# Decode attention with a gated MLP on one core: the output summed transposed, wo on 32 partitions, and the last V in 64-row pieces

## The chip, the core and the metric

The kernel runs on one NeuronCore of a Trainium2 chip. The metric is the device time of one execution in microseconds (us). A core has a matrix engine (PE, whose weight loads the profile lists as PEld), a vector engine (DVE), a scalar engine (ACT), a general engine (POOL) and a queue engine (SP) that here issues transfers only. Sixteen DMA engines move data between HBM and the on-chip memory of 128 partitions; each engine works through its own packets in order.

## What is computed

The input is one token for each of two batches. A branch "a" is attention over a cache of 16,384 keys and values for 32 heads of 128 elements; a branch "b" is a mixer and an MLP; a gate mixes the two. With S = 1 the mixer's shifted groups are all zero, which the kernel uses (`shT` is zero).

```python
x = A_x                                            # 2 x 1 x 1024
g = sigmoid((x * gate_w).sum(-1, keepdims=True))
q = (x @ wq) by heads                              # 2 x 32 x 1 x 128
p = softmax(q k^T * 128**-0.5)                     # k_cache: 2 x 32 x 16384 x 128
a = (p @ v_cache) by heads @ wo                    # wo: 4096 x 1024
x1 = Bx + shifted(gelu(layernorm(Bx) @ w1)) @ w2
b = x1 + gelu(layernorm(x1) @ w3) @ w4             # w3: 1024 x 3584
out = g * a + (1 - g) * b                          # bf16
```

(The branch "b" is given x as its input.) K and V are 537 MB of the 573 MB that are read.

## The kernel before

**Units.** The work is cut into 32 units: 16 pairs of heads (`HP`) times two batches (`s`). A unit reads 8 MB of K and 8 MB of V, each in one transfer of 128 partitions with 65,536 B in each (`unit_rows`). The buffer `mem` has five cells of 32 KB a partition: K of batch 0 lies in cells 0 and 1, K of batch 1 in cells 1 and 2, V in cells 3 and 4. K of the next unit may be loaded when the half of K that shares its cell has been transposed (`tr3`), V when the product with the V before it is done (`pvd`).

**One unit.** DVE transposes K in eight chunks into two buffers `kt` (L631); PE multiplies each chunk with the stationary query in 8 matmuls (L654). DVE transposes the scores (L638) and takes the maximum (L640); ACT spreads it into a diagonal `Dm` (L668), PE sums that to all partitions (`R`, L666), DVE takes the bias `nb` (L689), ACT the exponent (L674), PE the sum (L692), DVE its reciprocal (L694). The product with V of the unit before (`pe_pv`, L699: 64 matmuls of 512 moving columns) stands between L666 and L692 on PE. `dve_rows` (L747, L753) folds its four blocks into `red`, two matmuls (L717) turn `red` into a column form `ot`, and DVE copies it to `OT` (L782).

**The projection.** After the unit of batch 1, `pe_project` (L732) multiplies with the 256 rows of wo that belong to the pair of heads. wo lies as `wo_t`, 128 partitions by 2 rows of 1,024; `OT` is stationary (2 columns), wo is moving, and the output accumulates in `arow` as four groups of two rows with 256 columns, over all 16 pairs. `wod` marks it done, and SP waits for that before it loads the next wo (L874).

**The order on the queues.** SP issues all large transfers, in program order, each behind its wait: in the loop (L858 and on, 15 passes) K of batch 0, V of batch 0, wo, K of batch 1, V of batch 1. V and wo belong to the pass before. Each engine runs its instructions in the order written, with waits on counting semaphores; no planner reorders them.

**Before the loop** the branch "b" is computed, its parts set between the first two units: wq, w1, w2, K, w3, K, w4 are loaded in this order; the GELU after w3 (`gelu_T`, L468 to L496) follows unit 0's softmax and sum; the product with w4 (L510) stands before the last chunk of unit 1's scores; then the first `pvd` and `wod` are given by PE (L839, L840) behind unit 1's sum, and four row adds (L845) make `brow`.

**After the loop** the last V of batch 1 comes in nine pieces (L898): seven of 32 rows of V in each partition and two of 16. The first three pieces go through the form with V moving (24 matmuls L699), the other 160 rows through a form with V stationary and two moving columns (L952). The last 256 rows of wo come as `wo_l` in two transfers (L905). Then follow `OTl` (L958), 8 projection matmuls (L963), the add of `brow` (L970) and two stores of 4 rows, one on SP and one on ACT (L973).

## Time and profile before

| what | value |
|---|---|
| runs | 1334.83, 1335.35, 1336.12 us; median 1335.35 |
| profiled execution | 1336.33 us, its span 1334.6 us |
| read from HBM | 572.53 MB, 429 GB/s over the span |
| busy | PE 748.9 us (56%), PEld 302.2 (23%), DVE 710.5 (53%), ACT 104.6 (8%), POOL 12.4 (1%) |
| K transposes, L631 | 256 of 2,283 ns |
| score matmuls, L654 | 2048 of 418 ns |
| PV matmuls, L699 | 2008 of 384 ns |
| projection matmuls, L732 | 120 of 314 ns |
| wo transfers | 15 of 512 KB, 28.5 us from issue to landing (median) |
| K and V transfers of 8 MB | 28.3 and 30.9 us from issue to landing (median) |

Busy times are added over instructions; PE's and PEld's overlap. The time from issue to landing holds the wait behind earlier transfers in the queue. The span is from the first to the last instruction of the profile.

### The profile page before, as it was taken

How to read it: one execution, taken by the hardware profiler on the slowest of the kernel's cores; microseconds unless marked ns; L12 is line 12 of the kernel's file. 1: busy time of each engine (PE TensorE's matmuls, PEld its weight loads, DVE VectorE, ACT ScalarE, POOL GpSimd, SP SyncE). 2: the span in 40 equal slices, each digit the busy share in tenths (PEclk: the TensorE clock that was granted, in tenths of full speed). 3: DMA queues.
4: the chain of work that ended last, by engine and by line, in shares of the span. 5: the costliest groups of instructions: out<-in, count | busy, mean ns of one | idle time of the engine just before them, and what ended most of it. 6: DMA issues, size and time to landing. Idle time of an engine off the chain costs nothing.

```text
span 1334.6 us, 11800 instructions
## 1 busy us (share of the span) xinstructions
PE 748.9 (56%) x4920; PEld 302.2 (23%) x4920; DVE 710.5 (53%) x712; ACT 104.6 (8%) x164; POOL 12.4 (1%) x44
## 2 busy tenths in 40 slices
PE   0655666554566555466654546655455665555664
PEld 0222222222222222222222212222222222222222
DVE  1465565654556654456565445655444656545561
ACT  0010000000000000000000000000000000000000
POOL 0000000000000000000000000000000000000000
PEclk9778887777888777788777788877778877777886
DMA  9999999999999999999999999999999999999997
GB/s 409 437 419 425 431 433 432 430 438 430 434 432 434 432 432 438 426 438 430 434 432 434 436 428 438 428 436 431 434 438 428 436 428 438 424 441 436 430 436 317
DMA packets 13993, 572.68 MB, mean 429 GB/s; under 512 B 1936, under 2 KB 1952, under 8 KB 4384
## 3 DMA queue, kind: packets, MB, share of 16 engines
q1 hardware_dynamic: 13544, 572.53, 99.5%
q8 instruction: 8, 0.13, 0.0%
q10 hardware_dynamic: 440, 0.01, 0.0%
q14 instruction: 1, 0.01, 0.0%
HBM read 572.53 MB, written 0.00 MB: 429 GB/s over the span
## 4 chain that ended last, share of the span: by engine, by line
DMA 65%; DVE 16%; PE 12%; issue 5%; SPq 1%; POOL 0%; ACT 0%; POOLq 0%; ACTq 0%
DMA mem<-in_A_k_cache_dram 64%; DVE kt L631 15%; PE S L654 11%; DMA wo_last<-in_A_wo_dram 2%; SPq L898 1%; PE oacc L699 0%; PE oacc L510 0%; ACT pt L674 0%; SPq L905 0%; SPq L869 0%; DVE x1row L809 0%; DVE st L638 0%; POOL ln_rstd L450 0%; POOL qw L265 0%; DVE tsc L823 0%
## 5 line engine op out<-in xcount | busy, mean ns | idle before, releaser
L654 PE MATMUL S<-kt,qw 128*128 128x512 bf16 x2048 | 548.9, 418 | 306.8 <-DVE kt L631 306.7
L631 DVE STREAM_TRANSPOSE kt<-mem 128x2048 f32<-128x2048 f32 x256 | 570.7, 2283 | 208.0 <-DMA mem<-in_A_k_cache_dram 154.6
L654 PEld LDWEIGHTS S<-kt,qw 128*128 128x128 bf16 x2048 | 196.3, 104 | 645.7 <-issue 338.9
L699 PE MATMUL oacc<-mem,pt 128*8 128x512 bf16 x2008 | 115.9, 384 | 4.0 <-DMA mem<-in_A_v_cache_dram 4.0
L674 ACT ACTIVATE pt<-st,nb 64x256 bf16<-64x256 f32 x64 | 89.7, 1401 | 226.0 <-DVE nb L689 225.5
L747 DVE TENSOR_SCALAR part<-oacc,maskr 128x128 f32<-128x128 f32 x31 | 10.9, 351 | 143.0 <-PE oacc L699 143.0
L668 ACT ACTIVATE Dm<-ident_s,m 128x128 f32<-128x128 f32 x32 | 12.8, 401 | 921.2 <-DVE m L640 921.2
L692 PE MATMUL tot<-rs,lmat 128*128 128x1 f32 x64 | 18.7, 362 | 105.3 <-ACT pt L674 105.3
L694 DVE RECIPROCAL rinv<-tot 128x1 f32<-128x1 f32 x32 | 5.4, 168 | 113.1 <-PE tot L692 113.1
L699 PEld LDWEIGHTS oacc<-mem,pt 128*8 128x8 bf16 x2008 | 46.2, 87 | 61.3 <-DMA mem<-in_A_v_cache_dram 4.1
L638 DVE STREAM_TRANSPOSE st<-S 128x512 f32<-128x512 f32 x32 | 22.9, 717 | 69.8 <-PE S L654 69.8
L717 PE MATMUL ot<-hsel,red 128*128 128x2 f32 x120 | 19.0, 263 | 54.7 <-DVE red L753 54.7
L666 PE MATMUL R<-Dm,ones_f 128*128 128x128 f32 x64 | 15.6, 326 | 54.4 <-ACT Dm L668 54.4
L692 PEld LDWEIGHTS tot<-rs,lmat 128*128 128x128 f32 x64 | 16.0, 311 | 112.3 <-ACT pt L674 112.3
L717 PEld LDWEIGHTS ot<-hsel,red 128*128 128x128 f32 x120 | 16.4, 196 | 69.8 <-DVE red L753 69.8
L674 ACT ACTIVATION_READ_ACCUMULATOR pt<-st,nb 64x1 f32 x64 | 30.6, 478 | 0.0
L666 PEld LDWEIGHTS R<-Dm,ones_f 128*128 128x128 f32 x64 | 9.5, 188 | 70.2 <-ACT Dm L668 70.2
L753 DVE SCALAR_TENSOR_TENSOR part<-oacc,maskr,part 128x128 f32<-128x128 f32 x62 | 21.7, 351 | 2.2
L782 DVE CAST OT<-ot 64x2 bf16<-64x2 f32 x60 | 9.6, 160 | 22.2 <-PE ot L717 21.8
L344 PE MATMUL tot<-zp,ones_f 128*128 128x2 f32 x2 | 0.6, 364 | 33.7 <-DVE zp L366 33.7
L615 POOL TENSOR_TENSOR qw<-qd,mask 128x16 bf16<-128x16 f32 (+1 forms) x32 | 8.4, 263 | 1138.6 <-PE S L654 1138.6
L689 DVE TENSOR_REDUCE nb<-R 64x1 f32<-64x64 f32 x64 | 14.2, 222 | 3.4 <-PE R L666 2.1
(104 smaller groups left out, 116.0 us busy)
## 6 DMA issues: line engine op xcount, KB each, us to landing
mem<-in_B_w_dram SPq DMA_DIRECT2D x2, 7168.0 KB, 27.6
wo<-in_A_wo_dram SPq DMA_DIRECT2D x15, 512.0 KB, 28.5
mem<-in_A_v_cache_dram SPq DMA_DIRECT2D x7, 1024.0 KB, 18.4
mem<-in_B_w_dram SPq DMA_DIRECT2D x2, 2048.0 KB, 29.3
mem<-in_A_v_cache_dram SPq DMA_DIRECT2D x2, 512.0 KB, 27.7
mem<-in_A_k_cache_dram SPq DMA_DIRECT2D x32, 28.3
wo_last<-in_A_wo_dram SPq DMA_DIRECT2D x2, 256.0 KB, 21.6
mem<-in_A_v_cache_dram SPq DMA_DIRECT2D x31, 30.9
```

The costliest lines, as they stand in the source:

```text
L631: DVE.transpose(out=kt[n % 2][:], in_=k_view(s)[:, c * CT : (c + 1) * CT, :].rearrange("p j d -> p (j d)").bitcast(FP32),).then_inc(S(f"tr ...
L638: DVE.transpose(out=st[:].rearrange("p j r -> p (j r)"), in_=sps[s][:]).then_inc(S("stT"), 1)
L654: ins = PE.matmul(sps[s][:].rearrange("p (j k) -> p j k", k=QP), lhsT=qw[s][:, v, NG - 1 - m : NG - 1 - m + P], rhs=ktb[:, half * GT : (ha ...
L666: PE.matmul(R_ps[:, 0:P], lhsT=ones_f[:], rhs=Dm[:], start=True, stop=True).then_inc(S("rr"), 1)
L668: ACT.activation(out=Dm[:], in_=ident_s[:], func=ACTF.Copy, scale=m_t[:, 0:1]).then_inc(S("dm"), 1)
L674: ins = ACT.activation(out=pts[s][rows, :, e, :].rearrange("p (m a) k -> p a k m", a=GT // 4), in_=st[rows, :, 0:NG].rearrange("p (a k) m ...
L689: ins = DVE.tensor_reduce(out=nb_t[rows], in_=R_ps[rows, rows], axis=AX.X, op=ALU.min)
L692: PE.matmul(tot_ps[:, 0:1], lhsT=lmat[:], rhs=rs_t[:], start=True, stop=True).then_inc(S("tt"), 1)
L699: ins = PE.matmul(oacc[s][QP * q : QP * q + 8, :], lhsT=pts[s][:, g].rearrange("p h k -> p (h k)"), rhs=V[:, 4 * g : 4 * g + 4, :].rearran ...
L717: ins = PE.matmul(ot_ps[:, 2 * r : 2 * r + 2], lhsT=red[:].rearrange("p e d -> p (e d)")[:, r : 2 * Dh : 2], rhs=hsel[:], start=True, stop ...
L753: ins = DVE.scalar_tensor_tensor(out=red[:] if twice else part[:], in0=in0.unsqueeze(1).to_broadcast([P, 2, Dh]) if twice else in0, scalar ...
L898: SP.dma_start(out=region(V_CELL, NJ * Dh)[:, at * Dh : (at + size) * Dh], in_=unit_rows(v_rows, HP - 1, 1)[:, at * Dh : (at + size) * Dh] ...
```

## The change

- wo lies on 32 partitions with 8 rows of 1,024 each (`WP` = 32, `WR` = 8), still 512 KB a transfer. The temporary `tsc` now shares its memory.
- The projection has wo stationary (every eighth column, 32 x 128) and `OT` moving (two columns): 64 matmuls for 8. `OT` is made by 8 matmuls instead of 2 and by two dependent DVE steps with a selector `esel`. The output accumulates transposed, 128 partitions by 8 by 2.
- `brow` is built in the same layout from `x1T`; xrow with its two loads, the row adds and some memsets go. One store on ACT writes the output, in pieces of 16 B.
- The last V comes in pieces of 64, 64, 64, 32, 16, 16 rows; the first three (192 rows) go through the moving form. `wo_l` lies in cell 2 and waits for the last transposes.
- `softmax` and `total` are split in five steps. In the loop their order on each engine stays; before the loop GELU comes ahead of unit 0's exponent, unit 0's sum stands amid unit 1's scores, `pvd` is given right behind the w4 product, and `wod` by DVE's step that makes `brow`.

```diff
-    wo_t = sb([P, 2, D], BF16, "wo")
-    wo_l = sb([P, 2, D], BF16, "wo_last")
+    wo_t = sb([P, WR, D], BF16, "wo")
+    wo_v = wo_t[0:WP].rearrange("p r (n c) -> p r c n", c=KC)
-    tsc = sb([P, HQ * Dh], FP32, "tsc")
+    tsc = wo_t[:, 0:2, :].rearrange("p r n -> p (r n)").bitcast(FP32)
...
-    wo_rows = A_wo.rearrange("(g p r) n -> g (p r n)", p=P, r=2)
+    wo_rows = A_wo.rearrange("(g p r) n -> g (p r n)", p=WP, r=WR)
...
         def pe_pv(u):
...
-            for r in range(2):
+            for r in range(WR):
                 ins = PE.matmul(
-                    ot_ps[:, 2 * r : 2 * r + 2],
-                    lhsT=red[:].rearrange("p e d -> p (e d)")[:, r : 2 * Dh : 2],
+                    ot_ps[0:WP, 2 * r : 2 * r + 2],
+                    lhsT=red[:].rearrange("p e d -> p (e d)")[:, r : 2 * Dh : WR],
...
         def pe_project(u):
...
-            for r in range(2):
-                for k in range(Q4):
+            for r in range(WR):
+                for c in range(KC):
                     ins = PE.matmul(
-                        arow[k],
-                        lhsT=OT[:, r, :],
-                        rhs=wo_t[:, r, k * NQ : (k + 1) * NQ],
+                        arow[:, c, :],
+                        lhsT=wo_v[:, r, c, :],
+                        rhs=OT[:, r, :],
...
         def dve_pv_end(u):
...
+            DVE.tensor_scalar(
+                out=oa[:], in0=ot[:, 0, :], scalar1=esel[:, 0:1], scalar2=None, op0=ALU.mult
+            ).then_inc(S("oad"), 1)
+            wait(DVE, "oad", u.after(-1))
             wait(DVE, "wod", u.i)
-            for e in range(2):
...
+            DVE.scalar_tensor_tensor(
+                out=OT[:, :, s], in0=ot[:, 1, :], scalar=esel[:, 1:2], in1=oa[:], op0=ALU.mult, op1=ALU.add
+            ).then_inc(S("OTd"), 1)
...
-        softmax(u0)
-        total(u0)
+        spread_max(u0)
...
         gelu_T(columns(FC), h2T[:], FC, "g2", "h2T")
+        bias(u0)
+        exponent(u0)
         pool_unit(u1)
-        dve_scores(u1)
-        pe_scores(u1, 0, NCK - 1)
+        dve_scores(u1, 0, NCK // 2)
+        pe_scores(u1, 0, NCK // 2 - 1)
+        total(u0)
+        invert(u0)
+        dve_scores(u1, NCK // 2)
+        pe_scores(u1, NCK // 2 - 1, NCK - 1)
         linear(h2T, w4_v, FC, D, "h2T", "c3", [ot_ps[:]], ["ot"])
-        pe_scores(u1, NCK - 1)
-        softmax(u1)
-        total(u1)
         ln.wait("PE", [ln.writer["ot"]])
         PE.sem_inc(S("pvd"), 1)
-        PE.sem_inc(S("wod"), 1)
+        pe_scores(u1, NCK - 1)
+        spread_max(u1)
+        bias(u1)
+        exponent(u1)
...
-                    SP.dma_start(out=wo_t[:].rearrange("p r n -> p (r n)"), in_=wo_source(i - 1)).then_inc(S("wol"), 16)
+                    SP.dma_start(out=wo_t[0:WP].rearrange("p r n -> p (r n)"), in_=wo_source(i - 1)).then_inc(S("wol"), 16)
...
-        PIECES = [32] * 7 + [16] * 2
+        PIECES = [64, 64, 64, 32, 16, 16]
...
+        wo_l = region(2, 2 * D).rearrange("p (e n) -> p e n", e=2)
+        wo_c = wo_l.rearrange("p e (n c) -> p e c n", c=KC)
+        wait(SP, f"tr{NCK - 1}", 2 * HP)
...
-            for k in range(Q4):
+            for c in range(KC):
                 ins = PE.matmul(
-                    arow[k], lhsT=OTl[:, e, :], rhs=wo_l[:, e, k * NQ : (k + 1) * NQ],
+                    arow[:, c, :], lhsT=wo_c[:, e, c, :], rhs=OTl[:, e, :],
...
-        for b, queue in ((0, SP), (1, ACT)):
...
+        ACT.dma_start(out=out.rearrange("b s (p c) -> p (b s) c", c=KC), in_=out_T[:]).then_inc(S("st"), 16)
```

More of the change, by code (lines that the diff above doesn't have):

```diff
@@ L127 @@
     HQ = H // Q4
+    WR = 8
+    WP = 2 * Dh // WR
     assert NCK == 8 and NG <= QP and FC * QP == FQ and KC * QP == NQ
@@ L144 @@
     kt = [sb([P, CT * Dh // 2], FP32, f"kt{k}") for k in range(2)]
-    wo_t = sb([P, 2, D], BF16, "wo")
-    wo_l = sb([P, 2, D], BF16, "wo_last")
+    wo_t = sb([P, WR, D], BF16, "wo")
+    wo_v = wo_t[0:WP].rearrange("p r (n c) -> p r c n", c=KC)
     st = sb([P, GT, QP], FP32, "st")
     Dm = sb([P, P], FP32, "Dm")
-    tsc = sb([P, HQ * Dh], FP32, "tsc")
+    tsc = wo_t[:, 0:2, :].rearrange("p r n -> p (r n)").bitcast(FP32)
     xin = sb([P, B, KC], BF16, "xin")
-    xrow = sb([P, NQ], BF16, "xrow")
     gwT = sb([P, KC], BF16, "gwT")
@@ L175 @@
     h2T = sb([P, FC, B], BF16, "h2T")
-    x1row = sb([P, NQ], FP32, "x1row")
-    brow = sb([P, NQ], FP32, "brow")
+    brow = sb([P, KC, B], FP32, "brow")
     g_rep = sb([P, B], FP32, "g_rep")
-    omgrow = sb([P, 1], FP32, "omgrow")
+    omg = sb([P, B], FP32, "omg")
+    esel = sb([WP, 2], FP32, "esel")
     m_t = sb([P, 1], FP32, "m")
@@ L188 @@
     red = sb([P, 2, Dh], FP32, "red")
-    OT = sb([P, 2, B], BF16, "OT")
+    oa = sb([WP, WR], FP32, "oa")
+    OT = sb([WP, WR, B], BF16, "OT")
     OTl = sb([P, 2, B], BF16, "OT_last")
-    out_row = sb([P, NQ], BF16, "out_row")
+    out_T = sb([P, B, KC], BF16, "out_T")
     sps = [psum.tile([P, GT * QP], FP32, name=f"S{k}") for k in range(2)]
@@ L195 @@
     oacc = [oacc2[:, k, :] for k in range(2)]
-    arow_t = psum.tile([P, NQ], FP32, name="arow")
-    arow = [arow_t[QP * k : QP * k + B, :] for k in range(Q4)]
+    arow = psum.tile([P, KC, B], FP32, name="arow")
     R_ps = psum.tile([P, 2 * P], FP32, name="R")
@@ L220, in wo_source @@
         flat = wo_rows[hp : hp + 1, :] if isinstance(hp, int) else wo_rows[bass.ds(hp, 1), :]
-        return flat.rearrange("o (p x) -> (o p) x", p=P)
+        return flat.rearrange("o (p x) -> (o p) x", p=WP)
     ln = Line(nc, S)
@@ L248 @@
         ln.dma("ACT", gwT[:], gate_w.rearrange("(p r) -> p r", p=P), "l_gw", writes=["gwT"])
-        for b in range(B):
-            ln.dma(
-                "ACT", xrow[b : b + QP * (Q4 - 1) + 1 : QP, :],
-                A_x[b, 0].rearrange("(k n) -> k n", k=Q4), f"l_xr{b}", writes=[f"xrow{b}"],
-            )
         ln.op("POOL", lambda: POOL.memset(ident_f[:], 0.0), writes=["ident"])
@@ L273 @@
         ln.op("DVE", lambda: DVE.memset(ot_ps[:], 0.0), writes=["ot"])
-        ln.op("DVE", lambda: DVE.memset(arow_t[:], 0.0), writes=["arow"])
         ln.op("DVE", lambda: DVE.memset(shT[:], 0.0), writes=["shT"])
-        ln.op("DVE", lambda: DVE.memset(brow[:], 0.0), writes=["brow"])
         ln.op("DVE", lambda: DVE.memset(hm2[:], 0.0), writes=["hm2"])
@@ L330 @@
         )
+        ln.op(
+            "DVE",
+            lambda: DVE.tensor_reduce(
+                out=esel[:], in_=ident_f[0:WP, 0:WP].rearrange("p (h k) -> p h k", h=2), axis=AX.X, op=ALU.add
+            ),
+            reads=["ident"], writes=["esel"],
+        )
         def many(count, make, reads, writes):
@@ L356, in compute_gate @@
             th = sb([P, B], FP32, "th")
-            om = sb([P, B], FP32, "om")
             ln.op(
@@ L383, in compute_gate @@
                 lambda: DVE.tensor_scalar(
-                    out=om[:], in0=g_rep[:], scalar1=-1.0, scalar2=1.0, op0=ALU.mult, op1=ALU.add
+                    out=omg[:], in0=g_rep[:], scalar1=-1.0, scalar2=1.0, op0=ALU.mult, op1=ALU.add
                 ),
-                reads=["g_rep"], writes=["om"],
-            )
-            ln.op(
-                "DVE",
-                lambda: DVE.tensor_tensor(out=om[:], in0=om[:], in1=rep1[:, 0:B], op=ALU.mult),
-                reads=["om", "rep1"], writes=["om"],
-            )
-            ln.op(
-                "DVE", lambda: DVE.tensor_reduce(out=omgrow[:], in_=om[:], axis=AX.X, op=ALU.add),
-                reads=["om"], writes=["omgrow"],
+                reads=["g_rep"], writes=["omg"],
             )
@@ L573 @@
         many(
-            Q4,
-            lambda g: PE.matmul(
-                arow[g],
-                lhsT=shT[:, 0, :],
-                rhs=rep4[:].rearrange("p g m -> p (g m)")[:, 0:NQ],
+            1,
+            lambda n: PE.matmul(
+                arow[:].rearrange("p c b -> p (c b)"),
+                lhsT=rep4[:, 0, :],
+                rhs=shT[:].rearrange("p c b -> p (c b)"),
                 start=True,
@@ L661, in pe_scores, with spread_max, exponent @@
                 ins.then_inc(S(f"sc{n}"), 1)
-        def softmax(u):
-            s = u.s
+        def spread_max(u):
+            wait(ACT, "mx", u.after(1))
+            ACT.activation(out=Dm[:], in_=ident_s[:], func=ACTF.Copy, scale=m_t[:, 0:1]).then_inc(S("dm"), 1)
             wait(PE, "dm", u.after(1))
             PE.matmul(R_ps[:, 0:P], lhsT=ones_f[:], rhs=Dm[:], start=True, stop=True).then_inc(S("rr"), 1)
-            wait(ACT, "mx", u.after(1))
-            ACT.activation(out=Dm[:], in_=ident_s[:], func=ACTF.Copy, scale=m_t[:, 0:1]).then_inc(S("dm"), 1)
+        def exponent(u):
+            s = u.s
             wait(ACT, "nbd", u.after(1))
@@ L682, in softmax, with bias @@
             ins.then_inc(S("ex"), 1)
-        def total(u):
-            s = u.s
+        def bias(u):
             wait(DVE, "rr", u.after(1))
@@ L690, in total, with invert @@
             ins.then_inc(S("nbd"), 1)
+        def total(u):
             wait(PE, "ex", u.after(1))
             PE.matmul(tot_ps[:, 0:1], lhsT=lmat[:], rhs=rs_t[:], start=True, stop=True).then_inc(S("tt"), 1)
+        def invert(u):
             wait(DVE, "tt", u.after(1))
-            DVE.reciprocal(out=rinv[s][:], in_=tot_ps[:, 0:1]).then_inc(S("rcp"), 1)
+            DVE.reciprocal(out=rinv[u.s][:], in_=tot_ps[:, 0:1]).then_inc(S("rcp"), 1)
         def pv_moving(V, s, g0, g1, ng):
@@ L778, in dve_pv_end @@
             wait(DVE, "otd", u.after(-1))
-            wait(DVE, "wod", u.i)
-            for e in range(2):
-                rows = slice(e * HALF, (e + 1) * HALF)
-                ins = DVE.tensor_copy(
-                    out=OT[rows, :, s],
-                    in_=ot_ps[rows, 0:4].rearrange("p (r e) -> p e r", e=2)[:, e],
-                )
-            ins.then_inc(S("OTd"), 1)
+            ot = ot_ps[0:WP, 0 : 2 * WR].rearrange("p (r e) -> p e r", e=2)
+            DVE.tensor_scalar(
+                out=oa[:], in0=ot[:, 0, :], scalar1=esel[:, 0:1], scalar2=None, op0=ALU.mult
+            ).then_inc(S("oad"), 1)
+            wait(DVE, "oad", u.after(-1))
+            wait(DVE, "wod", u.i)
+            DVE.scalar_tensor_tensor(
+                out=OT[:, :, s], in0=ot[:, 1, :], scalar=esel[:, 1:2], in1=oa[:], op0=ALU.mult, op1=ALU.add
+            ).then_inc(S("OTd"), 1)
         w3_v = region(3, KC * F).rearrange("p (r n) -> p r n", n=F)
@@ L790, with mark @@
         half = FQ // 2
+        def mark(ins, name):
+            ins.then_inc(S(name), 1)
+            return (S(name), 1)
         u0, u1 = Unit(0, 0), Unit(0, 1)
@@ L797 @@
         ln.wait("ACT", [ln.writer["ident_s"], ln.writer["pt0"], ln.writer["pt1"]])
-        ln.wait("PE", [ln.writer["lmat"], ln.writer["hsel"]])
+        ln.wait("PE", [ln.writer["lmat"], ln.writer["hsel"], ln.writer["esel"]])
         dve_scores(u0, 0, NCK // 2)
@@ L804 @@
         layernorm_T(x1T[:], xn2T[:], "ln2", "x1T", "xn2T")
-        for g in range(Q4):
-            rows = slice(QP * g, QP * g + B)
-            ln.op(
-                "DVE",
-                lambda rows=rows: DVE.tensor_tensor(
-                    out=x1row[rows, :], in0=ot_ps[rows, :], in1=xrow[rows, :], op=ALU.add
-                ),
-                reads=["ot", "xrow0", "xrow1"], writes=["x1row"],
-            )
         dve_scores(u0, NCK // 2)
@@ L829 @@
         gelu_T(columns(FC), h2T[:], FC, "g2", "h2T")
+        bias(u0)
+        exponent(u0)
         pool_unit(u1)
-        dve_scores(u1)
-        pe_scores(u1, 0, NCK - 1)
+        dve_scores(u1, 0, NCK // 2)
[4 more added lines that the diff above has]
+        pe_scores(u1, NCK // 2 - 1, NCK - 1)
         linear(h2T, w4_v, FC, D, "h2T", "c3", [ot_ps[:]], ["ot"])
-        pe_scores(u1, NCK - 1)
-        softmax(u1)
-        total(u1)
         ln.wait("PE", [ln.writer["ot"]])
         PE.sem_inc(S("pvd"), 1)
-        PE.sem_inc(S("wod"), 1)
-        for g in range(Q4):
-            rows = slice(QP * g, QP * g + B)
-            ln.op(
-                "DVE",
-                lambda rows=rows: DVE.tensor_tensor(
-                    out=brow[rows, :], in0=ot_ps[rows, :], in1=x1row[rows, :], op=ALU.add
-                ),
-                reads=["ot", "x1row"], writes=["brow"],
-            )
+        pe_scores(u1, NCK - 1)
+        spread_max(u1)
+        bias(u1)
+        exponent(u1)
+        ln.op(
+            "DVE", lambda: DVE.transpose(out=tsc[:, 0:NQ], in_=psum_rows(ot_ps[:], KC)),
+            reads=["ot"], writes=["tsc"],
+        )
+        ln.op(
+            "DVE", lambda: DVE.tensor_tensor(out=brow[:], in0=columns(KC), in1=x1T[:], op=ALU.add),
+            reads=["tsc", "x1T"], writes=["brow"], mark=lambda ins: mark(ins, "wod"),
+        )
+        total(u1)
+        invert(u1)
         ln.op(
             "DVE",
-            lambda: DVE.tensor_scalar(
-                out=brow[:], in0=brow[:], scalar1=omgrow[:, 0:1], scalar2=None, op0=ALU.mult
+            lambda: DVE.tensor_tensor(
+                out=brow[:], in0=brow[:], in1=omg[:].unsqueeze(1).to_broadcast([P, KC, B]), op=ALU.mult
             ),
-            reads=["brow", "omgrow"], writes=["brow"],
+            reads=["brow", "omg"], writes=["brow"],
         )
@@ L878 @@
                 pe_scores(u)
-                softmax(u)
+                spread_max(u)
                 pe_pv(u)
@@ L883 @@
                     pe_project(u)
+                bias(u)
+                exponent(u)
                 total(u)
-        landed = [f"l_{x}" for x in ("wq", "w1", "w2", "x", "gw", "xr0", "xr1", "w3", "w4")]
-        landed += [f"l_v31_{n}" for n in range(3)]
+                invert(u)
+        landed = [f"l_{x}" for x in ("wq", "w1", "w2", "x", "gw", "w3", "w4", "v31", "wo0", "wo1")]
         def landing(n):
-            return 32 if n < 9 else 16
-        PIECES = [32] * 7 + [16] * 2
+            return 32 if n < 7 else 16
+        PIECES = [64, 64, 64, 32, 16, 16]
         wait(SP, "tr3", 2 * HP)
@@ L940 @@
             wait(PE, landed[n + 1], landing(n + 1))
-            ins = pv_moving(V, 1, n * 8, (n + 1) * 8, moving // 4)
+            ins = pv_moving(V, 1, n * 16, (n + 1) * 16, moving // 4)
         ins.then_inc(S("pvd"), 1)
@@ L968 @@
         wait(DVE, "wod", HP + 1)
-        used = slice(0, QP * (Q4 - 1) + B)
-        DVE.tensor_tensor(out=out_row[used, :], in0=arow_t[used, :], in1=brow[used, :], op=ALU.add).then_inc(S("fin"), 1)
-        for b, queue in ((0, SP), (1, ACT)):
-            wait(queue, "fin", 1)
-            queue.dma_start(
-                out=out[b, 0].rearrange("(k n) -> k n", k=Q4),
-                in_=out_row[b : b + QP * (Q4 - 1) + 1 : QP, :],
-            ).then_inc(S(f"st{b}"), 16)
-        for b in range(B):
-            wait(POOL, f"st{b}", 16)
+        DVE.tensor_tensor(
+            out=out_T[:].rearrange("p b c -> p c b"), in0=arow[:], in1=brow[:], op=ALU.add
+        ).then_inc(S("fin"), 1)
+        wait(ACT, "fin", 1)
+        ACT.dma_start(out=out.rearrange("b s (p c) -> p (b s) c", c=KC), in_=out_T[:]).then_inc(S("st"), 16)
+        wait(POOL, "st", 16)
 _INS = ['A_x', 'A_k_cache', 'A_v_cache', 'A_wq', 'A_wo', 'B_x', 'B_w1', 'B_w2', 'B_w3', 'B_w4', 'gate_w']
```

## The prediction

> **What bounds the kernel.** I read the page from the top. Part 2 says whether the memory stream ever stops, part 3 which queue carries it:

> ```profile
> DMA  9999999999999999999999999999999999999997
> GB/s 409 437 419 425 431 433 432 430 438 430 434 432 434 432 432 438 426 438 430 434 432 434 436 428 438 428 436 431 434 438 428 436 428 438 424 441 436 430 436 317
> ...
> q1 hardware_dynamic: 13544, 572.53, 99.5%
> ```

> The reader is to see a constant: every slice but the last is full, and SP's queue q1 alone keeps the 16 DMA engines busy for 99.5% of the span. The trace's record of each DMA packet says the same more sharply. From the first packet at 2.45 us to 1320 us the sixteen engines together stood idle for 0.6 us, 0.33 of it near 105 us and 0.06 near 123 us. Section 5's large waits (PE 306.8 us for DVE, DVE 154.6 us for K) are waits of engines that are faster than the stream. So the span is: 2.45 us to the first packet, 1,327.8 us of packets, and from the last landing (1330.2 us) the tail. Only three things can move the time: the time of the packets, a hole in the stream, and the tail.

> Next the SP queue's own waits (us in total, times, longest), to see whether a hole is near:

> ```profile
> SPq L869 <- DVE kt L631: 605.0, 30, 22.9
> SPq L871 <- PE oacc L699: 464.1, 29, 16.0
> SPq L874 <- PE arow L732: 40.8, 14, 3.1
> ```

> SP waits for half of K's transposes (L869), for PV (L871), for the projection (L874). What matters is how early each issue still is. Setting the issue times beside the packet records, K of unit 0 is issued at least 5.1 us before the first engine runs dry (from the second pass on), K of unit 1 6.2, V 7.9, wo 23.9. Before the loop it is closer: 1.6 us at 103.33 and 2.1 us at 122.52, and these two are the holes above; so about 2 us of lead are needed, and the steady loop has 3 to 4 us over.

> **wo on 32 partitions, the term that decides.** Now: 15 transfers of 128 packets of 4,096 B, eight to an engine. A packet is recorded with 0.159 us and the next begins 0.155 us after it: 8 x 0.155 = 1.24 us of each engine for one transfer. After: 32 packets of 16,384 B, two to an engine. The weights w1 and w2 already have such packets: 0.613 us, next after 0.609. So 2 x 0.609 = 1.22 us, if an engine goes on at its pace. That end is -0.02 us each, -0.3 us in all.

> But whose pace is it? K's packet of 65,536 B takes 2.42 us: 27.1 GB/s an engine, 433 GB/s for sixteen, and the GB/s row agrees. All large transfers shown cover all 128 rows, each engine writing eight of its own. No row shows two engines writing into one engine's eight rows, so the trace cannot say whether 27.1 GB/s is what an engine gives or what its rows take. If rows take it, the worst end is a quarter: 32 of 128 rows at 4 x 27.1 GB/s, 524,288 B in 4.84 us, +3.6 us each, +54 us. Between lies half: 8 x 27.1 = 217 GB/s, 2.42 us, +1.18 us each, 15 x 1.18 = **+17.7 us**. I take half: the row of K's packets is as near to the one end as to the other, and half is the middle of the three. Nothing hides it: the rows that wo reaches are the same that K and V fill in the same stream, which is full, so bytes added to their share lengthen it, whatever the other engines do meanwhile.

> [...]

> **V pieces.** 56 packets of 8,192 B an engine (next after 0.309 us) become 24 of 16,384 and 8 of 8,192: 17.30 us becomes 17.09, **-0.2 us**.

> **Before the loop.** GELU's chain (90.21 to 92.8 us) now comes before the exponent and its sum; DVE no longer waits 3.5 us for the sum ahead of it, so unit 1's transposes start when its K has landed (about 90.3 us) and not at 92.93. K's issue at 103.33 comes some 2.5 us earlier. V's first issue waited 18.7 us for PE's mark behind the sum (L839); the mark now follows the w4 product (done at 114.8), some 8 us earlier. Both holes close: **-0.4 us**. The queue-order risk is wo, which waits for the new brow step; it stands behind V with 21.9 us of lead.

> **The loop's compute.** PE gets 8 `ot` matmuls of 32 columns for 2, and 64 projection matmuls with wo stationary for 8. The timeline of PE and DVE around 200 us (start, duration, engine and line, idle time before and its releaser) shows the gap that they fall into:

> ```profile
> 199.22 0.39 PE L732 MATMUL arow<-wo,OT 128*2 128x256 bf16 x8 [0.52 <-DVE OT L782]
> ...
> 203.10 0.17 DVE L694 RECIPROCAL rinv<-tot 128x1 f32<-128x1 f32 x1 [3.54 <-PE tot L692]
> 207.32 4.50 DVE L631 STREAM_TRANSPOSE kt<-mem 128x2048 f32<-128x2048 f32 x2 [4.05 <-DMA mem<-in_A_k_cache_dram]
> 209.78 5.76 PE L654 MATMUL S<-kt,qw 128*128 128x512 bf16 x16 [6.71 <-DVE kt L631]
> ```

> `ot`: 4 PE instructions took 0.63 us; 16 cost 1.0 to 2.5, so OT is 0.4 to 1.9 us later. Projection: nearest are L952's pairs with a full stationary and two moving columns, 32 in 0.95 us: 64 are 1.9 us. L952's weight load alone is 0.104 us: 6.7 us. Load and matmul end to end (0.140 + 0.165) are 19.5 us. I take 2 to 7, since these pairs are what L952 runs; that it reads every eighth element matters little where L717 (every second, 196 ns) stands beside L933 (dense, 188). The projection then ends between 202 and 208.5 us, the sum's matmul behind it on PE and DVE's reciprocal by 209, and DVE's transposes behind that reciprocal are at most some 2 us late, inside the 4 us of K's lead: 0. Behind wod waits SP with wo, then K of unit 1, which waits until 218 us anyway. DVE's two OT steps replace two of 0.16 us: 0.

> **The tail**, from the same view (PEld is PE's weight load):

> ```profile
> 1328.98 0.59 PE L952 MATMUL R<-pt,mem 128*128 128x2 bf16 x16 [0.65 <-DMA mem<-in_A_v_cache_dram]
> ...
> 1330.26 0.09 PEld L963 LDWEIGHTS arow<-wo_last,OT_last 128*2 128x2 bf16 x4 [0.34 <-DMA wo_last<-in_A_wo_dram]
> 1330.69 0.42 DVE L970 TENSOR_TENSOR out_row<-arow,brow 98x256 bf16<-98x256 f32 x1 [0.92 <-PE arow L963]
> 1331.15 0.67 SPq L973 DMA_DIRECT2D out_dram<-out_row  x1
> ```

> Now the last landing sets it. After, rows 0 to 191 go through the moving form, and row 191 lands at 1323.98; 16 moving matmuls (1.7 us at the halved clock, from 64 in 5.67), DVE's four steps (1.64, from 1318.39 to 1320.03), then 0.3 and 64 L952 matmuls in three blocks (1.0, 0.6, 0.6) reach 1330.1 instead of 1329.57. Then 16 matmuls with wo stationary (0.5 to 1.7) instead of waiting to 1330.26: the add starts at 1330.85 to 1332.1 against 1330.69. The add on 128x16 is 0.17 (L591) instead of 0.42; the store drops SP's transfer, whose packets ended 0.4 us after ACT's, but writes pieces of 16 B (the 16 B packets of xin took 9 ns each). Bounds -0.5 to +0.8; I take **+0.2**. The new wait for the last transposes (1289.4) is over before V's pieces are issued. The dropped xrow loads, memsets and row adds sit beside the stream: 0.

> **Sum.** 17.7 - 0.2 - 0.4 + 0.2 = +17.3 us. The profiled execution took 1336.33 us (span 1334.6, 1.7 around it), which makes 1353.6; the median shown is 0.98 lower, so I predict 1352.7.

> **Rivals.**
> 1. *The rows take the full rate* (not slower). The engines are the limit, wo costs -0.3, the rest -0.4: -0.7 us, 1334.6. For it: packets run at one pace at every size from 4,096 to 65,536 B, as an engine's own limit would. Against: each of them had its rows to itself. It decides at the transfer's rate: above 369 GB/s (1.42 us, 15 x 0.18 = 2.7 us) the loss is under 0.2%, which is about what a measurement here can tell from no change. The case that wo is still cut into 4 KB pieces ends here too. Chance 0.30.
> 2. *A quarter of the rate*: 1352.7 + 15 x 2.42 = 1389. Chance 0.03.
> 3. *PE becomes late*: strided stationaries at 19.5 us end the projection near 221; the first scores come some 11 us late, K's lead is gone by about 6 us, holes of 15 x 6 = 90 us, 1425; at 11 us of projection nothing yet. Against: L717. Chance 0.04.
> 4. *Faster by over 0.2%*: tail and holes together would have to give 2.7 us; the slowest engine lands 1.3 us behind the third slowest, partly an instruction fetch of 1.1 us that may fall elsewhere. Chance 0.03.

> The forecast has 0.60. Its own range is 1350 to 1357 (tail -0.5 to +0.8, the fetch 1.1 either way, wo 1.1 to 1.35 us a transfer). Since 0.33 lies at or under the old time, the 8-in-10 range reaches down to rival 1 with its tail: 1333.5 to 1357. Faster 0.03, within 0.2% 0.30, slower 0.67.

> **What would show it.** Right: wo's 16,384 B packets near 1.2 us instead of 0.61, part of the K and V packets beside them longer than 2.42, the loop's period 1.2 us longer, DMA still at 9 in all slices. Wrong: packets at 0.61 and the same period (rival 1); idle DMA before K of unit 1 (rival 3). The holes near 105 and 123 us should be gone in any case; a tail over 1.5 us longer would refute my tail.

## The result and the profile after

| | before | after |
|---|---|---|
| runs, us | 1334.83 to 1336.12 (4), median 1335.59 | 1374.19, 1391.23, 1396.56, 1399.13, median 1393.89 |
| profiled execution (span), us | 1336.33 (1334.6) | 1399.13 (1397.4) |
| period of the loop, from one first wo packet to the next, us | 78.7 | 82.7 |

The ratio is 1.035 with a 95% interval of 1.024 to 1.046, some 47 us by it; the comparison leaves out the two longest runs of after, one of them the profiled one, and the stretch explained below is seen just so in shorter runs of kernels with the same loss. The forecast was +17 us. The sign was right, the size was not, and the time is outside the range of 1333.5 to 1357.

The page of after, parts 2 and 3 (40 slices of the span; queue: packets, MB, share of 16 engines):

```profile
DMA  9999999999999999999999999999999999999996
GB/s 420 419 443 423 396 426 401 424 403 426 441 385 439 377 435 396 409 430 373 435 390 401 446 398 424 401 418 404 414 431 400 400 401 422 407 416 422 400 424 269
...
q1 hardware_dynamic: 11664, 572.53, 98.6%
```

The reader is to see two things that seem at odds. The engines are still "busy" in every slice, yet they move 373 to 446 GB/s where before moved 419 to 441, in every slice from the second to the last but one. The same 572.53 MB takes 62.8 us longer. Most of that is packets that became longer, and 10.4 us an engine is idle time. The record of each packet gives the sum (us for each of the 16 engines, profiled executions):

| where | before | after | more |
|---|---|---|---|
| wo's 15 transfers, packets | 18.6 | 32.7 | +14.1 |
| packets of 65,536 B (K, V), time over 2.422 each | 2.7 | 40.0 | +37.3 |
| idle from the first packet to the end of the loop | 0.5 | 8.1 | +7.6 |
| idle at the end | 4.9 | 7.7 | +2.8 |
| V pieces | | | -0.2 |

That is 61.6 of 62.8 us. wo's packets of 16,384 B take 1.09 us (median 1.2); V's pieces and w, with packets of the same size, stay at 0.613. Of 8,192 packets of 65,536 B, 812 are now longer than 2.5 us, the longest 5.6; before it was 63. Over 15 passes wo's own packets cost 0.94 us a pass, their neighbours 2.5, the idle time 0.5: together the 4.0 by which the period grew.

These are means, and the idle time is not spread evenly. The first four passes take 81.8 to 81.9 us, 3.2 more than before, and the engines hardly stop in them; around the first wo transfer K and V already lose 2.3 us. From the sixth pass on the period is 82.3 to 84.7 us, and nearly all of the 8.1 us of idle time lies there, most of it ahead of K of batch 0. SP's issues of that K, one of before, then an early and a later one of after, from their timelines:

```profile
730.20 0.34 SPq L869 DMA_DIRECT2D mem<-in_A_k_cache_dram  x1
```

```profile
181.14 0.33 SPq L865 DMA_DIRECT2D mem<-in_A_k_cache_dram  x1
...
764.38 0.33 SPq L865 DMA_DIRECT2D mem<-in_A_k_cache_dram  x1
```

By the packet records the first packet of that K starts 5.2 us after the issue in before and 5.2, 5.1, 4.7, 4.2 and 2.6 us in the first five passes of after. In the later passes it is 1.0 to 1.4 us, with engines idle by then: the lead is gone. Meanwhile the engines drift apart. The first and the last of them reach wo about 4 us apart in the first pass and 9 to 10 us apart in the later ones, so the first to finish needs the next K early, while the transposes that free its memory wait for the last.

The windows view of after around one wo transfer, that of the longest pass (84.7 us), shows the place (stretch in us, its length, busy time and count on PE, PEld, DVE, ACT and POOL, clock, DMA share, GB/s; the last two count a packet by where it starts, so a long packet raises the share of the window that it starts in):

```profile
553.00:556.00 3.00, 2.72 (x13) 0.98 (x11) 3.00 (x2) 0.00 (x0) 0.00 (x0) 1.00 1.51 360
556.00:559.00 3.00, 2.44 (x12) 0.85 (x11) 2.67 (x2) 0.00 (x0) 0.00 (x0) 1.00 0.60 137
559.00:562.00 3.00, 1.64 (x8) 0.54 (x6) 1.29 (x3) 0.12 (x1) 0.27 (x1) 1.00 1.05 289
562.00:565.00 3.00, 1.55 (x14) 0.68 (x18) 0.05 (x1) 0.29 (x1) 0.00 (x0) 0.68 0.84 317
553.00:565.00 12.00, 8.36 (x43) 3.05 (x45) 7.01 (x6) 0.40 (x1) 0.27 (x1) 0.92 1.00 276
```

Over these 12 us the engines are fully busy (1.00) at 276 GB/s. Nothing waits for an issue in this stretch; the stream itself is slow.

Compute is not the cause. The timeline of after shows PE and DVE in the same gap that the prediction showed of before (start, duration, engine and line, idle time before and its releaser):

```profile
531.80 3.98 PE L727 MATMUL arow<-OT,wo 32*128 32x2 bf16 x64 [0.65 <-DVE OT L780]
...
536.33 0.17 DVE L689 RECIPROCAL rinv<-tot 128x1 f32<-128x1 f32 x1 [4.31 <-PE tot L685]
539.33 4.50 DVE L621 STREAM_TRANSPOSE kt<-mem 128x2048 f32<-128x2048 f32 x2 [2.84 <-DMA mem<-in_A_k_cache_dram]
```

The 64 matmuls take 3.98 us, DVE's reciprocal follows, and DVE then still waits 2.84 us for K. Of SP's waits (us in total, times, longest) only the one for the projection ahead of wo grows by much in total, from 40.8 to 99.0 us, 7.1 at the longest; the one for PV stands at 468.5 where it was 464.1:

```profile
SPq L865 <- DVE kt L621: 604.7, 30, 28.0
SPq L867 <- PE oacc L694: 468.5, 29, 20.1
SPq L870 <- PE arow L727: 99.0, 14, 7.1
```

### The profile page after: what moved, and what is told of

The parts are those of the page before. It is cut to its first block, busy times and chain, and to the rows that moved or that the text cites. A ratio compares the mean times of both kernels' runs of the same rounds, so it can differ in the third digit from the quotient of the medians.

```text
span 1397.4 us, 14048 instructions
## 1 busy us (share of the span) xinstructions
PE 817.6 (59%) x6053; PEld 372.8 (27%) x6053; DVE 707.4 (51%) x703; ACT 106.1 (8%) x164; POOL 12.4 (1%) x44
## 3 DMA queue, kind: packets, MB, share of 16 engines
q1 hardware_dynamic: 11664, 572.53, 98.6%
HBM read 572.53 MB, written 0.00 MB: 410 GB/s over the span
## 4 chain that ended last, share of the span: by engine, by line
DMA 69%; DVE 15%; PE 11%; issue 4%; another core or an unknown queue 0%; POOL 0%; SPq 0%; ACT 0%; POOLq 0%
DMA mem<-in_A_k_cache_dram 67%; DVE kt L621 15%; PE S L644 10%; DMA mem<-in_A_v_cache_dram 2%; PE oacc L694 0%; PE ot L500 0%; SPq L865 0%; PE R L953 0%; PE arow L964 0%; POOL qw L260 0%; POOL pt L262 0%; SPq L896 0%; DVE st L628 0%; DVE part L748 0%
## 5 line engine op out<-in xcount | busy, mean ns | idle before, releaser
L694 PE MATMUL oacc<-mem,pt 128*8 128x512 bf16 x2032 | 122.9, 397 | 7.0 <-DMA mem<-in_A_v_cache_dram 7.0
L666 ACT ACTIVATE pt<-st,nb 64x256 bf16<-64x256 f32 x64 | 91.2, 1425 | 246.1 <-DVE nb L680 245.6
L712 PE MATMUL ot<-hsel,red 128*32 128x2 f32 x480 | 34.4, 202 | 54.7 <-DVE red L748 54.7
L694 PEld LDWEIGHTS oacc<-mem,pt 128*8 128x8 bf16 x2032 | 47.6, 89 | 69.5 <-DMA mem<-in_A_v_cache_dram 9.1
L727 PE MATMUL arow<-OT,wo 32*128 32x2 bf16 x960 | 59.7, 193 | 9.7 <-DVE OT L780 9.7
L727 PEld LDWEIGHTS arow<-OT,wo 32*128 32x128 bf16 x960 | 58.9, 164 | 10.6 <-issue 10.6
L712 PEld LDWEIGHTS ot<-hsel,red 128*32 128x32 f32 x480 | 31.8, 157 | 69.8 <-DVE red L748 69.8
L685 PEld LDWEIGHTS tot<-rs,lmat 128*128 128x128 f32 x64 | 15.9, 307 | 62.0 <-ACT pt L666 61.6
L775 DVE TENSOR_SCALAR oa<-ot,esel 32x8 f32<-32x8 f32 x30 | 6.4, 214 | 37.2 <-PE ot L712 37.2
```

The costliest lines, as they stand in the source:

```text
L666: ins = ACT.activation(out=pts[s][rows, :, e, :].rearrange("p (m a) k -> p a k m", a=GT // 4), in_=st[rows, :, 0:NG].rearrange("p (a k) m ...
L685: PE.matmul(tot_ps[:, 0:1], lhsT=lmat[:], rhs=rs_t[:], start=True, stop=True).then_inc(S("tt"), 1)
L694: ins = PE.matmul(oacc[s][QP * q : QP * q + 8, :], lhsT=pts[s][:, g].rearrange("p h k -> p (h k)"), rhs=V[:, 4 * g : 4 * g + 4, :].rearran ...
L712: ins = PE.matmul(ot_ps[0:WP, 2 * r : 2 * r + 2], lhsT=red[:].rearrange("p e d -> p (e d)")[:, r : 2 * Dh : WR], rhs=hsel[:], start=True, ...
L727: ins = PE.matmul(arow[:, c, :], lhsT=wo_v[:, r, c, :], rhs=OT[:, r, :], start=False, stop=False, skip_group_check=True,)
```

## The experiments

The theory formed on this: **A**, the 32 rows take their bytes at less than the stream's rate, and what they lack falls on the neighbours too (A8: at half of it, over rows 0 to 63 no faster than over 0 to 31; Ap: in proportion to the rows; A4: at a quarter). "Entrance" in the expectations names whatever limits these rows; it is an assumption, and no run shows what it is. Rivals: **B**, PE's longer `ot` and projection make K late; **C**, another part of the change; **C2**, the packets' size, two to an engine in place of eight. All edits are made in the kernel after, unless said.

**1. wo over all 128 partitions, the rest of the change kept.**

```diff
-    WR = 8
+    WR = 2
```

> All of the change, but wo lies on 128 partitions with 2 rows each (128 packets of 4,096 B a transfer, 16 projection matmuls, 2 matmuls for ot). Theory A (the 32 rows are a narrow entrance, and everything else is worth about nothing): no packet longer than in the kernel before, 1334.6 us, between 1333.5 and 1336.5. Theory B (PE's longer ot and projection make the loop late): with 16 instead of 64 projection matmuls also near 1335, so this run does not part A from B. Theory C (something else of the change, the new order before the loop or the tail, costs tens of us): above 1350.

Measured: 1333.53 us (1333.32 to 1333.73) against 1336.02, ratio 0.998 (0.997 to 0.999). The whole loss is in wo's layout or what hangs on it (C falls), and the rest of the change gains 2.5 us. The holes account for some of that. Windows of before, then of this kernel:

```profile
118.00:130.00 12.00, 1.07 (x4) 0.80 (x4) 4.06 (x9) 3.13 (x5) 0.00 (x0) 0.67 0.93 377
```

```profile
118.00:130.00 12.00, 1.86 (x6) 0.97 (x7) 4.23 (x6) 2.44 (x4) 0.00 (x0) 0.50 1.00 431
```

The idle times near 105 and 123 us add up to only 0.39 us, but the packets that come right after them were longer as well, by 1.19 us an engine before and 0.08 here. The last landing falls from 1330.23 to 1327.56 us; from it to the span's end there are 4.3 us in both.

**2. 32 rows, but every fourth partition.** 64 projection matmuls, 32 packets of 16,384 B, two to an engine, as in after; only the rows that wo lands on differ. DVE clears wo's memory first, and the projection reads mostly zeros, so its output leaves wo's part out.

```diff
-SP.dma_start(out=wo_t[0:WP]...
+SP.dma_start(out=wo_t[0:P:4]...
```

> The changed kernel, but each wo transfer writes its 32 rows of 16,384 B into every fourth of the 128 partitions instead of partitions 0 to 31. The projection reads partitions 0 to 31 as before, so it multiplies with rows that are mostly zero; its instructions and waits stay. [...] Theory B (PE): unchanged, 1374 to 1399. Theory C2 (the size of the packets, two to an engine, is at fault): unchanged, 1374 to 1399.

Measured: 1333.30 us (1333.24 to 1333.57), ratio 0.998 (0.997 to 0.999). wo's packets take 0.61 us. Windows of this kernel with its wo packets at 536.8 to 539.6 us:

```profile
535.00:538.00 3.00, 2.72 (x13) 1.05 (x12) 3.00 (x2) 0.00 (x0) 0.00 (x0) 1.00 1.00 431
538.00:541.00 3.00, 2.72 (x13) 0.92 (x11) 1.19 (x1) 0.00 (x0) 0.00 (x0) 1.00 1.02 442
541.00:544.00 3.00, 1.30 (x19) 0.68 (x22) 1.33 (x3) 0.40 (x1) 0.26 (x1) 1.00 0.96 415
```

No trace of a dip. The packets have the same count, size and source, and the compute is the same: C2 and B fall together, and A is left: what decides here is which rows are written.

**3. All 128 rows, with the 64-matmul projection.** wo's bytes land as before; the projection reads the first 32 rows and zeros, so its output is not that of wo.

```diff
-SP.dma_start(out=wo_t[0:WP]...
+SP.dma_start(out=wo_t[:, 0:2, :]...
```

> The changed kernel, but each wo transfer writes 128 rows of 4,096 B as in the kernel before. The projection keeps its 64 matmuls and reads partitions 0 to 31 of that memory, so it multiplies with other rows of wo; its instructions and waits stay. Theory A and theory C2: 1333 to 1337 us. Theory B (PE): unchanged, 1374 to 1399.

Measured: 1333.69 us (1333.28 to 1333.94), ratio 0.998 (0.997 to 0.999). The view of the tile wo (min, median, max ns; first and last start) shows that the compute is after's, 960 matmuls for the 240 of experiment 1:

```profile
L728 PE MATMUL arow<-OT,wo x960: 192/193/198, 197.1 to 1302.9; 32*128 32x2 bf16 x192
```

So B falls by itself, too.

**4. 32 rows, every second of 64.** As experiment 2, with `wo_t[0:HALF:2]`; wo's part is left out in the same way.

> The changed kernel, but each wo transfer writes its 32 rows into every second partition from 0 to 62; the projection multiplies with rows that are partly zero, its instructions and waits stay. [...] Theory A in the form of a share that grows with the rows spanned (64 of 128 instead of 32): about half of the loss, 1350 to 1365. Theories B and C2: unchanged.

Measured: 1381.56 us (1376.26, 1386.87), ratio 1.034 (1.030 to 1.038), as bad as after and above the 1350 to 1365 of a share that grows with the rows spanned. Its page at 1386.87 us, and below it that of experiment 2:

```profile
GB/s 411 436 423 434 394 425 405 424 408 425 433 399 430 403 430 427 406 443 384 439 392 432 432 393 433 396 426 403 426 432 399 430 394 414 410 436 414 403 424 272
```

```profile
GB/s 410 435 423 433 447 420 443 423 437 431 435 431 435 431 435 435 431 435 433 433 433 433 439 429 437 429 437 431 437 437 429 437 429 437 425 441 427 441 425 330
```

The first row has dips like after's, down to 384 in the loop; the second stays at 420 or more from the second slice to the last but one. Here K and V lose 31.8 us an engine over before and idle time 4.7, wo 14: the same three parts at a smaller total, with less idle time (10.4 in after). In the loop it lies in the last two passes only. wo's packets take 1.09 us in this kernel as in after, where experiment 2 has 0.61: rows spread over 0 to 63 are written no faster than rows 0 to 31.

**5. 64 partitions, 4 rows of wo each.** The whole computation is kept.

```diff
-    WR = 8
+    WR = 4
```

> All of the change, but wo lies on 64 partitions (0 to 63) with 4 rows each, 32 projection matmuls. [...] Theory Ap (the loss goes with the number of rows written, half as many bytes a row): 1345 to 1362.

Measured: 1382.78 us (1372.18, 1393.38) against 1336.42. Twice the rows and packets half the size. The two runs lie 21 us apart, but the shorter one too is 35.8 us over before and above the range of Ap (1345 to 1362): rows 0 to 63 cost about what rows 0 to 31 cost, as A8 has it, and Ap falls.

**6. Half of wo's bytes into partitions 0 to 31.** The second half of each wo transfer is left out, zeros in its place.

```diff
-SP.dma_start(out=wo_t[0:WP]...
+SP.dma_start(out=wo_t[0:WP, 0 : WR // 2, :]...
```

> The changed kernel with half of each wo transfer left out: 256 KB into partitions 0 to 31; the projection multiplies the other half with zeros, its instructions and waits stay. The stream is 15 x 0.61 = 9 us shorter by its bytes. If the loss goes with the bytes that crowd into the 32 rows: half of 41 to 63 us, less 9, so 1345 to 1356 us. If a transfer costs the same whatever its bytes: 1365 to 1390.

Measured: 1357.40 us (1353.9, 1360.9), ratio 1.016 (1.010 to 1.022), 1.4 us above the range that was expected for a loss in proportion to the bytes. K and V lose 20.3 us an engine over before where after has 37.3: 0.54 of it for half the bytes. The engines do not run dry in this kernel's loop.

**7. The transfer by itself.** The kernel of experiment 1, and behind its output eight groups of loads, each started when the one before has landed; the whole time is that of other work and is not compared.

> The kernel with wo on 128 partitions; after its store, when nothing else moves, eight groups of transfers are added, each waiting for the one before: 512 KB of wo into 128 partitions, into partitions 0 to 31, into every fourth of 128, into every second of 64, into 64 to 95, into 16 partitions; then 2 MB of V, wo, 2 MB of V back to back, with wo into every fourth of 128 and into 0 to 31. Theory A8: alone, packets of 16,384 B last 1.22 us (half rate, 217 GB/s) in 0 to 31, every second of 64 and 64 to 95, 0.61 us in every fourth of 128; 32,768 B in 16 partitions 4.8 us (a quarter). Theory A4 (a quarter for 32 rows): 2.4 us in 0 to 31, 1.2 in every second of 64. In the last two groups: if only wo's packets pay, V's of 16,384 B stay at 0.61 and the group is 1.2 us longer; if the neighbours pay too, as in the loop of the changed kernel, V's packets reach 1 us and more and the group is 2 us or more longer.

512 KB, from the first packet's start to the last one's end:

| rows | us | GB/s | packet, median us |
|---|---|---|---|
| 128 | 2.42 | 217 | 0.16 (4,096 B) |
| every 4th of 128 (32) | 1.83 | 287 | 0.74 |
| 0 to 31 | 2.62 | 200 | 1.12 |
| every 2nd of 64 (32) | 2.58 | 204 | 1.20 |
| 64 to 95 | 2.61 | 201 | 1.11 |
| 0 to 15 | 4.32 | 121 | 3.62 (32,768 B) |

Each starts from rest, and alone even the 128 rows stay far under the 433 GB/s of the stream, at 217, though their packets are as short as there. The three narrow targets of 32 rows (0 to 31, every 2nd of 64, 64 to 95) take 200 to 204 GB/s, about half of the stream's rate, as the prediction had it. The packets of 0 to 15 take 3.62 us where a quarter of the rate would give the 4.8 that was expected. With 2 MB of V ahead of it and behind it, the spread form takes 11.93 us and the narrow one 13.21: **+1.3 us**, close to the forecast's 1.18, not the 3.2 to 4.4 of the loop. Something in the loop is missing here. Three candidates: **L**, in the loop the engines do not reach wo at the same time; **S**, K's and V's larger packets; **F**, something that builds up over the passes.

**8. A lead for some engines.** Groups of 8 MB of V, wo, 4 MB of V; in two groups, two loads of 8 rows, 8 packets each for the 16 engines, go ahead.

> The kernel with wo on 128 partitions; after its store six groups are added, each waiting for the one before: 8 MB of V, 512 KB of wo into 32 partitions, 4 MB of V, back to back. wo goes into every fourth of 128 partitions (spread) or into 0 to 31 (narrow). Groups 3 and 4 have two transfers of 8 rows of 32,768 B ahead, which only eight engines carry, so that eight engines come 2.4 us later to wo than the others. Theory L (the loss beyond 1.2 us a pass comes from engines that meet wo at different times: one that is away from its entrance leaves it idle, and later shares it): narrow minus spread is 1.2 to 1.5 us without the lead and 2.5 to 4 us with it. Theory S (it comes from the size of the K and V packets beside it, 65,536 B): 2.5 to 4 us in both. Theory F (it needs the steady loop's feedback, buffers that free later): 1.2 to 1.5 us in both.

From the first wo packet to the end, spread against narrow: 11.36 and 11.43 against 13.08 and 13.79 without a lead (+1.7 and +2.4), 12.01 against 15.52 with it (+3.5). Without a lead that is more than the 1.2 to 1.5 that L and F expected, and less than the 2.5 to 4 of S: the large packets alone do not bring the 4 us. The lead does move the price. It was weak, though: in the spread form the engines reached wo only 1.1 us apart where 2.4 was meant. I put that down to the time that the issues take (0.35 to 0.48 us each in experiment 7's timeline); that is an estimate.

**9. The lead between V and wo, in three sizes, each pair twice.**

> As the run with a lead, but the lead (0, 2 or 4 transfers of 8 rows of 32,768 B, 1.2 us each on eight engines) stands between the 8 MB of V and wo, so that it is not lost in the time of the issues: 0, 2.4 and 4.8 us between the two halves of the engines. Each pair, spread and narrow, is there twice. Narrow minus spread, from the first wo packet to the end of the group: theory L (engines that meet wo at different times lose more): 1.0 to 2.4 us without a lead, 2.5 to 4 us with 2.4, 3 to 4.5 us with 4.8. Theory S or F: 1.0 to 2.4 us in all.

| lead of half the engines, as meant | spread, us | narrow, us | narrow costs |
|---|---|---|---|
| none | 11.51, 11.60 | 13.34, 13.57 | +1.8, +2.0 |
| 2.4 us | 13.49, 13.57 | 17.47, 17.27 | +4.0, +3.7 |
| 4.8 us | 18.96, 18.61 | 22.16, 22.66 | +3.2, +4.1 |

The packets tell which term grows. wo's own lose 1.0 to 1.3 us an engine in all rows; V's beside them lose 0.8 without a lead, about 2.4 with 2.4 us and 2.5 with 4.8, all as narrow minus spread. These are the loop's two numbers, 0.94 and 2.5. So the neighbours' loss needs nothing that builds up over the passes, and S falls; the idle time of the later passes is the part that F names. Two limits of this experiment: with the lead of 4.8 us the engines reach wo 7.3 to 7.5 us apart in the spread form, whose own V packets lose 2.3 us there; and the two loads of the 2.4 us lead write rows of partitions 0 to 63, over which wo was as slow as over 0 to 31 in experiments 4 and 5 (1381.56 and 1382.78 us). Ahead of the spread wo they cost V nothing (0.0 us), but whether being apart alone makes the narrow form dearer, or these bytes have a part in it, is not separated. L is thus supported, not isolated. In the loop's traces the first and the last engine end a transfer 6.4 us apart in after (median), 3.0 before, 2.0 to 2.2 in experiments 1 to 3: the narrow loads set the engines apart themselves. In the loop that shows as idle time in the later passes; K's and V's own loss is at 2.3 us in the first pass already.

**10. A version that beats both.** Experiment 1 with one less block in the moving form, to shorten the end.

```diff
-        PIECES = [64, 64, 64, 32, 16, 16]
+        PIECES = [64, 64, 32, 64, 16, 16]
```

> The kernel with wo on 128 partitions, and the last V in pieces of 64, 64, 32, 64, 16, 16 rows, the first three (160 rows) through the moving form. If the tail of the kernel with 192 moving rows is set by PE's and DVE's chain behind the third piece, as its timeline shows (OT_last at 1327.28, last landing 1327.56, projection until 1328.64), the projection starts by 1327.6 for its second half and the time falls by 0.3 to 0.6 us, to 1333.0. If the last landing sets it already: 1333.5 as before.

Measured: 1333.35 us (1333.21 to 1333.46) against 1335.82, ratio 0.998 (0.997 to 0.999); experiment 1 has the same ratio, so the 0.18 us between their medians is not shown, nor the fall of 0.3 to 0.6 that was expected. Their timelines, experiment 1 first:

```profile
1325.40 1.84 PE L953 MATMUL R<-pt,mem 128*128 128x2 bf16 x64
1327.28 0.16 DVE L959 TENSOR_TENSOR OT_last<-R,rinv_last 128x2 bf16<-128x2 f32 x1 [2.39 <-PE R L953]
...
1328.94 0.41 ACTq L974 DMA_DIRECT2D out_dram<-out_T  x1
```

```profile
1326.84 0.16 DVE L959 TENSOR_TENSOR OT_last<-R,rinv_last 128x2 bf16<-128x2 f32 x1 [5.59 <-PE R L953]
...
1328.50 0.41 ACTq L974 DMA_DIRECT2D out_dram<-out_T  x1
```

The store is issued 0.44 us earlier, in these two executions.

## Why the prediction was wrong

**The step that failed is "+1.18 us each, 15 x 1.18 = +17.7 us".** Its price of wo's own packets was near (0.94 a pass in the loop; with its neighbours +1.3 to +2.4 where the engines run together), and about half the rate was right (1.09 us a packet against 0.61; 200 GB/s alone). What failed is the sentence behind it: that wo's rows are full in the stream anyway, "so bytes added to their share lengthen it". That holds if those rows are never left idle, and then by the forecast's estimate 1.2 us is all a pass can lose. In the loop it lost 4.0: K's and V's packets beside wo took another 2.5 us an engine, and 0.5 went as idle time. The runs show that the 2.5 vanishes on other rows (experiment 2) and goes with the bytes (0.54 for half); that it comes with the engines being apart (0.8 when they are not) is supported by experiment 9, with the limits told there. The forecast named "part of the K and V packets beside them longer than 2.42" as a sign, and gave it no price.

**Rivals.** Full rate (0.30) fell: of the 32-row targets run in the loop (0 to 31, every second of 64, every fourth of 128) only the last has 0.61 us a packet. A quarter came near in time (1389) for a wrong reason: rows 0 to 31 take about half the rate (1.09 us a packet), and only 0 to 15 come near a quarter (121 GB/s alone). PE late (1425) fell by experiment 3. Faster fell for the change as a whole, though its other parts reach -2.5 us, just short of the 2.7 that this rival asked for.

**Holes, -0.4.** Right in place, mis-sized: with the stretched packets of the restart it is 0.39 + 1.19 - 0.08 = 1.5 us. I had counted the idle time alone.

**V pieces, -0.2**: -0.2. **Tail, +0.2**: about 0 in experiment 1 (4.3 us from the last landing, as before). In the profiled execution of after it is 5.8 us; its output store, issued at 1392.80 us, took some 1.5 us longer to land than that of experiment 1. Holes, pieces and tail make -1.7 of experiment 1's -2.5 us; the other 0.8 is not traced further.

**Compute at 0**: right. The projection took 3.98 us (forecast 2 to 7), `ot`'s 16 instructions 1.15 (1.0 to 2.5), and DVE still waited for K behind them. What the prediction did not foresee is that the lead of K's issue over its first packet, 5.2 us before, is used up in the later passes; that comes from the stream, for with the same 64 matmuls the period of experiment 3 stays at 78.7 us. **Signs**: longer wo packets, longer neighbours and DMA at 9 came as named; the period grew 4.0 us and not 1.2.

**Left open.** Why the neighbours stretch on all 16 engines and not on some (near each wo transfer of after, 15 or 16 packets longer than 2.5 us are in flight at once); what a stretched packet waits for; what sets the engines apart further from pass to pass; and why runs of narrow kernels differ (1374 to 1399, 1372 and 1393) when those of experiments 1 to 3 hold within 0.7 us. The profiled ones fit a start of the idle time that varies: about the sixth pass at 1399 us, the ninth at 1393 (experiment 5), the thirteenth at 1387 (experiment 4); no profile of the shortest runs was taken. That the crowded rows are left idle for part of the time is argued from the sum, not seen.

## What to carry to other kernels

In a kernel that is bound by its load stream, ask of each transfer which rows it lands on, and not only how many bytes it has: a narrow target slowed its neighbours in the stream here, and that was 2.5 of 4.0 us a pass. If data has to lie on 32 partitions, try them spread over the whole memory: every fourth cost nothing here (1333.30 us, against 1333.53 on all 128). And price a slow transfer in the loop itself: in a single pass with its engines in step it showed 1.3 to 2.4 us of the 4.0.
